# Two row tiles' transposes moved to DMA, with four smaller moves, in a kernel of attention and a gated MLP

## The chip, the core and the metric

The kernel runs on one core of one Trainium2 chip. The metric is the device time of one execution in microseconds (us). All executions told of here were in the same, fast state. Their mean granted TensorE clock was 0.998 or more of full speed, except in the slow executions of two experiments (0.995 to 0.998), whose profiles show TensorE standing still for over 6 us. "The first chunk", "chunk 1" and so on are four pieces of 512 tokens (numbers 0 to 3), each of four row tiles of 128 tokens.

## The reference, cut to what matters

```python
S, D, F = 2048, 1024, 3584
def reference(A_x, A_wqkv, A_wo, B_x, B_w_gate, B_w_up, B_w_down):
    x = A_x
    # attention: 32 heads of 32, each query looks at 8 keys spaced 2 apart
    h = x + attention(layernorm(x) @ A_wqkv) @ A_wo
    n = layernorm(h)
    return h + ((n @ B_w_gate) * (n @ B_w_up)) @ B_w_down
```

## The kernel before

The matrix products run back to back on TensorE. What they need is made by the other engines: layer norm on VectorE (`bn_stats`, then a normalization) with the reciprocal deviation from two small ScalarE instructions (`rs` in the traces); the transposed normalized rows `lnT` either through TensorE (`transpose_on_array`) or by a transposing DMA. The products' results land in PSUM tiles out of a pool of eight, and ScalarE copies each one out (`sg`).

```python
psum = ctx.enter_context(tc.tile_pool(name="psum", bufs=8, space=PSUM))
...
class Norm1:                                  # chunks 1, 2, 3
    def stat(self, t):
        stats(xtiles[self.c][t], self.mv4, t)         # VectorE
        rstd_of(self.mv4, self.rs4, t, t + 1)         # ScalarE: "rs"
    def norm(self, t):
        self.lns[t] = normalize(xtiles[self.c][t], self.mv4, self.rs4, t)
    def transpose(self, t):
        ...
        nc.sync.dma_start_transpose(lnTs[c][:, :, bass.ts(t, 128)], self.lns[t][:])
    def transpose_on_array(self, t):
        ...                                   # 8 TensorE transposes, then 2 copies PSUM -> lnT

def rows_gen(n, on_array):
    for t in range(6):
        if t < 4:
            n.stat(t)
            yield 1.5
        if 0 < t < 5:
            n.norm(t - 1)
            yield 0.55
        if t > 1 and on_array:
            n.transpose_on_array(t - 2)
            yield 0.45
...
def first_norm(t):                            # chunk 0, in two halves
    lns[t] = lnp.tile([128, D], BF, tag="ln", name=f"ln0_{t}")
    for i in range(2):
        cols = bass.ts(i, 512)
        nc.vector.tensor_scalar(lns[t][:, cols], x0[t][:, cols], mv0[:, t, 0:1], rs0[:, t:t + 1],
                                ALU.subtract, ALU.mult)
...
def evac_qkv(c, m, ps):
    sg = t1k.tile([128, HB + TC], BF, tag="t1k", name=f"sg{c}_{m}")
    nc.scalar.copy(sg[:, HB:HB + TC], ps[:])  # frees a PSUM tile
    ...
```

Side work such as the statistics is laid between the product groups by a small scheduler when the program is built: `bg.add(generator, ready)` lets a generator start once the planned time passes `ready`. The plan fixes the order of instructions on each engine; at run time each engine works in that order (ScalarE's 10 us of idling, shown further down, are an example). The stretch that will matter is this one.

```python
qkv(0, range(1, 4))
load_qk(0)                                    # query, then key rows of chunk 0, by GpSimd's DMA
bg.finish(rows2)
for t in range(4):
    norm1[2].transpose(t)                     # chunk 2, SyncE's DMA
xtiles[3] = load_x(3, "x", nc.sync)           # rows of chunk 3
pump(6)
bg.add(stats_gen(norm1[3]), bg.now + 6.0)     # their statistics
start_attention(0)
qkv(1, range(4))
```

The pair product near 520 us works from sums of weights (`sw`, out of the scaled weights `ws`) and of activations (`prodx`, out of `lnT`); the last stage, near 710 us, converts and subtracts f16 cells before the last down products.

```python
retire(1)
activation_sums(l2, l3, dn["px"])
weight_sums(0, nc.vector)
...
for k in range(NP):                           # NP = 14 cells of 128x512
    nc.vector.tensor_tensor(HF["21"][k], HF["11"][k], HF["21"][k], ALU.subtract)
for k in range(NP):
    nc.vector.tensor_tensor(HF["11"][k], S1[k], HF["11"][k], ALU.subtract)
sub(t2h, down["b22"], t1h)
```

## Time and profile before

| | before |
|---|---|
| time, median of 3 runs | 779.04 us (778.85 to 779.19) |
| span of the profiled execution | 777.6 us |
| TensorE busy | 770.7 us (99%) |
| VectorE, ScalarE, GpSimd busy | 614.9, 473.8, 142.3 us |
| TensorE idle inside the span | 6.9 us |

With TensorE busy 99% of the span, the other engines' shares say nothing by themselves. The list of TensorE's waits is the place to start, and each wait is then read in the timeline: a line there gives the start, the length, the engine, the source line (L), the operation, out<-in, and in brackets how long the engine had stood idle and what released it. One thing about those brackets was learned only later and is used below: a 512-column matmul is recorded as 0.38 us long, but in a full row the next one starts 0.22 us after it, so an idle time after a matmul leaves out 0.16 us of what was lost.

### The profile page before, as it was taken

The page shows a single profiled execution, that of the slowest core. Times are in us where ns is not written, and L with a number is a line of the kernel's source. Part 1 is how long each engine was busy: PE and PEld are TensorE (multiplying, and loading weights), DVE is VectorE, ACT ScalarE, POOL GpSimd, SP SyncE. Part 2 cuts the span into 40 slices and gives each one's busy share as a digit, 9 for nine tenths or more (in the row PEclk, how much of TensorE's full clock was granted, in tenths as well). Part 3 has the DMA queues.
Part 4 walks back from the last instruction along what each step waited for, and adds up shares of the span by engine and source line. Part 5 has one row for each costly group of instructions (what it writes and reads, how often), then busy time and mean ns, then how long its engine had stood idle before and what let it go on. Part 6 is the DMA issues. An engine that isn't in the chain of part 4 may idle for free.

```text
span 777.6 us, 10495 instructions
## 1 busy us (share of the span) xinstructions
PE 770.7 (99%) x3707; PEld 355.1 (46%) x3707; DVE 614.9 (79%) x805; ACT 473.8 (61%) x1029; POOL 142.3 (18%) x152
## 2 busy tenths in 40 slices
PE   8999999999999999999999999999999999999998
PEld 6544444444444444444444444444444444444444
DVE  6619999999899999999988989985553444579862
ACT  4627445323476661976769899746677677788240
POOL 0000000010000200002000001008778687600000
PEclk9999999999999999999999999999999999999999
DMA  8999693895965868867645384744332423730001
GB/s 275 258 217 222 158 291 88 255 305 130 338 205 167 269 228 239 267 225 259 207 150 192 120 298 121 162 96 111 106 97 67 109 62 101 248 131 28 1 27 55
DMA packets 181605, 133.86 MB, mean 172 GB/s; under 512 B 79024, under 2 KB 174384, under 8 KB 179504
## 3 DMA queue, kind: packets, MB, share of 16 engines
q1 hardware_dynamic: 176912, 110.12, 50.1%
q0 software_dynamic: 3584, 22.02, 8.1%
q10 hardware_dynamic: 1056, 1.05, 0.4%
q8 instruction: 29, 0.48, 0.3%
q14 instruction: 24, 0.20, 0.1%
HBM read 104.86 MB, written 22.02 MB: 163 GB/s over the span
## 4 chain that ended last, share of the span: by engine, by line
PE 88%; DVE 9%; DMA 1%; ACT 1%; issue 0%; SPq 0%; ACTq 0%; DVEq 0%
PE ps L392 20%; PE pg L392 12%; PE pu L392 12%; PE dx L787 6%; PE pz L680 6%; PE acc L626 6%; PE py L680 6%; PE px L680 6%; PE wo L513 4%; PE pv L680 3%; PE dy L787 3%; DVE h L834 1%; DMA w_qkv<-in_A_wqkv_dram 1%; PE ps L353 1%; PE ex L787 1%; DVE prodx L780 1%
## 5 line engine op out<-in xcount | busy, mean ns | idle before, releaser
L392 PE MATMUL ps<-lnT,w_qkv 128*128 128x512 bf16 x736 | 159.8, 379 | 0.0
L392 PEld LDWEIGHTS <-w_qkv 128*128 128x128 bf16 x736 | 71.8, 98 | 86.0 <-issue 0.3
L392 PE MATMUL pg<-lnT,w_wg 128*128 128x512 bf16 x448 | 105.8, 379 | 0.0
L392 PE MATMUL pu<-lnT,w_wu 128*128 128x512 bf16 x448 | 105.8, 379 | 0.0
L304 ACT CAST sg<-ps 128x512 bf16<-128x512 f32 x96 | 54.8, 590 | 52.7 <-PE ps L392 50.0
L475 DVE TENSOR_TENSOR pv<-vD,at 128x4096 bf16<-128x4096 bf16 x32 | 72.5, 2287 | 0.3
L432 DVE TENSOR_TENSOR prod<-qD,kD 128x4096 bf16<-128x4096 bf16 x32 | 72.3, 2284 | 0.1
L680 PEld LDWEIGHTS <-sw 128*128 128x128 f16 x448 | 43.8, 98 | 54.3 <-issue 1.7
L392 PEld LDWEIGHTS <-w_wg 128*128 128x128 bf16 x448 | 43.8, 98 | 52.9
L392 PEld LDWEIGHTS <-w_wu 128*128 128x128 bf16 x448 | 43.8, 98 | 52.9
L596 ACT CAST us<-pu 128x512 bf16<-128x512 f32 x56 | 33.2, 593 | 40.5 <-PE pu L392 40.4
L680 PE MATMUL px<-lnT,ws 128*128 128x512 bf16 x224 | 55.2, 379 | 0.0
L680 PEld LDWEIGHTS <-ws 128*128 128x128 f16 x336 | 32.9, 98 | 39.6
L626 PE MATMUL acc<-w_wd,gs 128*128 128x512 bf16 x224 | 48.5, 379 | 0.0
L487 POOL DMA_DIRECT2D od<-oD x4 | 2.2, 544 | 252.8 <-DVE oD L485 162.5
L661 POOL TENSOR_TENSOR sw<-ws 128x512 f16<-128x512 f16 x26 | 30.0, 1153 | 85.4 <-PE py L680 78.2
L185 ACT ACTIVATE rs<-mv,eps 128x1 f32<-128x1 f32 (+1 forms) x25 | 7.4, 297 | 52.6 <-DVE mv L182 49.2
L591 ACT CAST gs<-pg 128x512 bf16<-128x512 f32 x56 | 32.9, 587 | 10.7 <-PE pg L392 8.7
L434 DVE TENSOR_TENSOR prod<-prod 128x4096 bf16<-128x4096 bf16 x16 | 36.6, 2288 | 0.3
L541 ACT ACTIVATE junkd<-w_wd 128x512 bf16<-128x512 bf16 x56 | 34.3, 618 | 0.0
L626 PEld LDWEIGHTS <-gs 128*128 128x128 bf16 x224 | 21.9, 98 | 26.4
L697 ACT COPY py<-px 128x512 f32<-128x512 f32 x28 | 16.0, 570 | 26.2 <-PE px L680 26.2
(312 smaller groups left out, 1400.5 us busy)
## 6 DMA issues: line engine op xcount, KB each, us to landing
w_wg<-in_B_w_gate_dram SPq DMA_DIRECT2D x14, 1024.0 KB, 6.7
w_wu<-in_B_w_up_dram SPq DMA_DIRECT2D x14, 1024.0 KB, 5.4
w_wd<-in_B_w_down_dram SPq DMA_DIRECT2D x8, 896.0 KB, 8.8
w_pair<-in_B_w_gate_dram SPq DMA_DIRECT2D x14, 512.0 KB, 4.1
w_pair<-in_B_w_up_dram SPq DMA_DIRECT2D x14, 512.0 KB, 5.4
w_wo<-in_A_wo_dram SPq DMA_DIRECT2D x6, 1024.0 KB, 8.1
w_qkv<-in_A_wqkv_dram SPq DMA_DIRECT2D x5, 1024.0 KB, 9.1
kd<-sg SPq DMA_DIRECT2D x32, 144.0 KB, 3.0
```

The costliest lines, as they stand in the source:

```text
L304: nc.scalar.copy(sg[:, HB:HB + TC], ps[:])
L392: nc.tensor.matmul(ps[:], lhsT=wt[:, ko, bass.ts(j, 128)], rhs=rhs[:, ko, :], start=(ko == 0), stop=(ko == KO - 1))
L432: nc.vector.tensor_tensor(prod[:, j], qD[:], kD[:, :, o:o + SUB], ALU.mult)
L434: nc.vector.tensor_tensor(prod[:, :, 0:16], prod[:, :, 0:16], prod[:, :, 16:32], ALU.add)
L475: nc.vector.tensor_tensor(pv[:, j], vD[:, :, o:o + SUB], at[:, w, None, :].to_broadcast((128, DH, SUB)), ALU.mult)
L513: nc.tensor.matmul(ps[:], lhsT=oTs[c][:, kk, t, :], rhs=wts["wo", c, hf][:, kk, :], start=(kk == 0), stop=(kk == KO - 1))
L541: nc.scalar.activation(junk, src, ACTF.Abs, accum_out=self.l1[:, k:k + 1])
L591: nc.scalar.copy(gs[:], pg[:])
L596: nc.scalar.copy(us[:], pu[:])
L626: nc.tensor.matmul(acc[t][:], lhsT=hT[f][:, bass.ts(t, 128)], rhs=wts["wd", c, hf, b][:, j, :], start=(f == 0), stop=(f == NF - 1))
L680: nc.tensor.matmul(ps[:], lhsT=lhs[:, ko, :], rhs=rhs[:, ko, :], start=(fresh and ko == 0), stop=(ko == 3), skip_group_check=not fresh)
L787: nc.tensor.matmul(ps[:, bass.ds(lo, n)], lhsT=lhs[k][:, bass.ts(q, 128)], rhs=rhs[k][:, bass.ds(lo, n)], start=(fresh and k == 0), stop=( ...
```

## The change

Its intent is to take work and waits off TensorE's path at four places: sixteen transposes at 28 us, the first chunk's norm, the first pair product, and the last stage. Part 3 of the prediction is the weight half issued ahead of ScalarE's table load. The diff, with the repetitive end cut:

```diff
--- before.py
+++ after.py
@@ -222,11 +222,11 @@
         def norm(self, t):
             self.lns[t] = normalize(xtiles[self.c][t], self.mv4, self.rs4, t)
 
-        def transpose(self, t):
+        def transpose(self, t, eng=nc.sync):
             c = self.c
             if c not in lnTs:
                 lnTs[c] = lnTp.tile([128, KO, TC], BF, tag="lnT", name=f"lnT1_{c}")
-            nc.sync.dma_start_transpose(lnTs[c][:, :, bass.ts(t, 128)], self.lns[t][:])
+            eng.dma_start_transpose(lnTs[c][:, :, bass.ts(t, 128)], self.lns[t][:])
 
         def transpose_on_array(self, t):
             c = self.c
@@ -248,8 +248,11 @@
                 n.norm(t - 1)
                 yield 0.55
             if t > 1 and on_array:
-                n.transpose_on_array(t - 2)
-                yield 0.45
+                if t < 4:
+                    n.transpose_on_array(t - 2)
+                    yield 0.45
+                else:
+                    n.transpose(t - 2, nc.scalar)
 
     def stats_gen(n):
         for t in range(4):
@@ -278,8 +281,8 @@
     for t in range(4):
         load_x0(t)
     load_w0(0, 4)
+    load_w0(4, 4)
     nc.scalar.preload_act_table_set("natural_log_exp_and_others")
-    load_w0(4, 4)
     warm = t1k.tile([128, TC], BF, tag="t1k", name="warm")
     nc.vector.memset(warm[:], 0.0)
     eps = const.tile([128, 1], F32)
@@ -335,8 +338,7 @@
 
     def first_norm(t):
         lns[t] = lnp.tile([128, D], BF, tag="ln", name=f"ln0_{t}")
-        for i in range(2):
-            cols = bass.ts(i, 512)
+        for cols in (bass.ts(0, 512), bass.ts(1, 512)) if t == 0 else (slice(0, D),):
             nc.vector.tensor_scalar(lns[t][:, cols], x0[t][:, cols], mv0[:, t, 0:1], rs0[:, t:t + 1],
                                     ALU.subtract, ALU.mult)
 
@@ -977,8 +979,8 @@
         nc.vector.tensor_tensor(et[:], p5t[:, q, :], hs1[2 + q][:, 512:1024], ALU.add)
         result(1, hs1[2 + q], 2 + q, 1, ex[q], dn["inv"], et)
     retire(1)
+    weight_sums(0, nc.vector)
     activation_sums(l2, l3, dn["px"])
-    weight_sums(0, nc.vector)
     for q in range(2):
         dprod(ey[q], q, EF["12"], fcells(dn["22"]), False)
         nc.vector.tensor_tensor(p5t[:, q, :], p5t[:, q, :], hs1[q][:, 512:1024], ALU.add)
@@ -991,7 +993,8 @@
     for i in range(4):
         ht = hp.tile([128, D], BF, tag="h", name=f"hq_h{i}")
         h23 += [ht[:, 0:TC], ht[:, TC:2 * TC]]
-    for ht in (att.tile([128, KO, TC], BF, tag="oT", name="hq_o"), dn["lx"], dn["kx"], dn["vx"]):
+    rooms = (att.tile([128, KO, TC], BF, tag="oT", name="hq_o"), dn["lx"], dn["kx"])
+    for ht in rooms:
         h23 += [ht[:, k, :] for k in range(KO)]
 
 
@@ -1048,22 +1051,27 @@
     for q in range(4):
         nc.scalar.activation(ps_y[q][:], ps_x[q][:], ACTF.Copy, scale=sh)
     HF = {k: [f16(a) for a in HA[k]] for k in HA}
-    for k in range(NP):
-        to_f16(HF["22"][k], HA["22"][k], sh)
-        to_f16(HF["21"][k], HA["21"][k], sh)
+
+    GA = {k: HA[k][0:8] + [ht[:, r::4, :] for ht in rooms] for r, k in enumerate(("11", "21", "12", "22"))}
+    GF = {k: [f16(a) for a in GA[k]] for k in GA}
+    NG = len(GA["11"])
+    for k in range(NG):
+        to_f16(GF["22"][k], GA["22"][k], sh)
+        to_f16(GF["21"][k], GA["21"][k], sh)
     S1 = fcells(down["b11"])
-    for k in range(NP):
-        to_f16(HF["11"][k], HA["11"][k], sh, nc.scalar)
+    G1 = S1[0:8] + [f16(down["b11"][1][:, 2 * i + 1:2 * i + 3, :]) for i in range(3)]
+    for k in range(NG):
+        to_f16(GF["11"][k], GA["11"][k], sh, nc.scalar)
     conv_down(down["b22"], nc.scalar)
-    for k in range(NP):
-        nc.vector.tensor_tensor(S1[k], HF["21"][k], HF["22"][k], ALU.add)
+    for k in range(NG):
+        nc.vector.tensor_tensor(G1[k], GF["21"][k], GF["22"][k], ALU.add)
     for q in range(4):
         dprod(ps_x[q], q, HA["12"], fcells(down["b21"]), False)
         result(2, hs2[q], q, 0, ps_x[q], scale_d.inv, None)
-    for k in range(NP):
-        nc.vector.tensor_tensor(HF["21"][k], HF["11"][k], HF["21"][k], ALU.subtract)
-    for k in range(NP):
-        nc.vector.tensor_tensor(HF["11"][k], S1[k], HF["11"][k], ALU.subtract)
+    for k in range(NG):
+        nc.vector.tensor_tensor(GF["21"][k], GF["11"][k], GF["21"][k], ALU.subtract)
+    for k in range(NG):
+        nc.vector.tensor_tensor(GF["11"][k], G1[k], GF["11"][k], ALU.subtract)
     sub(t2h, down["b22"], t1h)
     p5 = []
     for q in range(4):
@@ (cut: HF["12"] likewise becomes GF["12"], over NG groups)
```

> **What bounds the kernel now.** I began with the first part of the page, the busy times, and then asked for the waits of TensorE alone, because the kernel looked as if one engine fills it.
>
> ```profile
> span 777.6 us, 10495 instructions
> PE 770.7 (99%) x3707; PEld 355.1 (46%) x3707; DVE 614.9 (79%) x805; ACT 473.8 (61%) x1029; POOL 142.3 (18%) x152
> ...
> PE 88%; DVE 9%; DMA 1%; ACT 1%; issue 0%; SPq 0%; ACTq 0%; DVEq 0%
> ```
>
> TensorE is busy for 770.7 of 777.6 us. The whole pool of idle time is 6.9 us (0.9% of the span), so no change that only removes waits can gain 2%. The chain of waits puts 9% on VectorE, and that can only be a place where VectorE ends a TensorE wait. The list of TensorE's waits says where:
>
> ```profile
> PE warm_ps L298 <- DVE warm L284: 1.2, 1, 1.2
> PE pv L680 <- DVE h L792: 1.1, 2, 0.9
> PE ps L353 <- ACT lnT L348: 0.3, 1, 0.3
> PE pt L347 <- DVE ln L340: 0.3, 1, 0.3
> PE ps L353 <- DMA w_qkv<-in_A_wqkv_dram: 0.3, 1, 0.3
> PE dy L787 <- DVE prodx L780: 0.3, 1, 0.3
> ```
>
> Three places are recoverable: the first token chunk (three waits of 0.3), the first pair product at about 520 us (1.1), and the last stage at 727 us (0.3 shown). The 1.2 at the start is not touched. From the end of the last matmul to the end of the span there are over 3 us of store, also untouched. So I read the timeline closely at exactly these places, and at 24 to 30 us, where the transposes of chunk 1 sit.
>
> **What the Trainium skill says.** (1) "DMA: Bandwidth & Descriptors", section "Silent corruption: two transposing streams in flight at once": transposes issued from the ScalarE queue and from the SyncE queue must not be in flight together; the later stream has to wait for the earlier one. Here the first SyncE transpose starts at 41.08 us, some 10 us after the new ScalarE ones would be issued, so if a wait is there it should be met already. The before trace has one stream only and cannot test this. (2) Same page, "Issuing engines are not separate DMA queues": another issuing engine buys no bandwidth, only sequencer time. So I give the choice of queue no transfer gain. (3) "Perfetto Trace Analysis", section "Optimizing Scalar/DVE Operations": about 60 ns overhead per VectorE instruction on SBUF, grouping helps where the engine is saturated, and splitting lets work end sooner where it only causes bubbles on others. The trace agrees on the size: near the end a pair of 128x512 f16 subtractions occupies 0.67 us from its start to the next pair's, and a 128x1024 one 0.61 us. (4) "TensorE: Matmul & The Clock Gate", "Part 4: PE-mode transpose" gives about 275 ns for a 128x128 transpose in one kernel. The trace differs in what a transpose costs in a row: eight of them push the next matmul by 0.45 us, 56 ns each; the measurement decides.
>
> **Part 1: two row tiles leave TensorE.** The chain of waits has these pieces:
>
> ```profile
> 24.72 1.73 PE ps L392 x8
> 26.90 1.73 PE ps L392 x8
> 28.62 0.89 PE ptb L238 x16
> ```
>
> Tiles 0 and 1 cost 0.45 us each between groups (24.72 + 1.73 = 26.45, next group at 26.90) and stay. Tiles 2 and 3 are the 16 transposes of 0.89 us, and they go: −0.89 us, directly on TensorE, which does not wait again before 519 us. Their four PSUM copies go too (two of 0.42 on VectorE, two of 0.59 on ScalarE), off the path. In their place ScalarE issues two DMA transposes. Estimated from SyncE's, each takes about 1.28 us to issue and 3.1 to 3.3 us to land:
>
> ```profile
> L229 SPq DMA_TRANSPOSE lnT<-ln x8: 1258/1280/5748, 41.1 to 94.9; - x8
> ...
> DMA to landing us min/median/max: 3.1/3.3/9.7
> ```
>
> The last norm of chunk 1 is done at 27.8 us and ScalarE has a cast and a copy before it, so issue from about 29.3, the second about 30.6, landed by about 34. The first chunk 1 matmul comes after twelve groups of 1.73 from 17.21 and the transposes: 17.21 + 20.7 + 0.45 + 0.45 + 0.89 = 39.7 before, 38.8 after. Slack of about 5 us.
>
> **Part 2: the first chunk's norm in one piece for tiles 1 to 3.** The normalization feeds the array's transposes:
>
> ```profile
> 13.88 0.73 DVE L340 TENSOR_SCALAR ln<-x,mv,rs 128x512 bf16<-128x512 bf16 x2 [0.86 <-ACT rs L186]
> 14.35 0.55 PEld L347 LDWEIGHTS <-ln 128*128 128x128 bf16 x8
> ...
> 14.79 1.07 ACT L348 COPY lnT<-pt 128x512 bf16<-128x512 bf16 x2 [0.94 <-PE pt L347]
> ```
>
> One half takes 0.41 us; 13.88 + 0.41 + 0.06 of signalling = 14.35, exactly when the transposes start. So they start on the first half. Tile 2 is alike: 11.44 + 0.41 + 0.06 = 11.91. One 128x1024 norm took 0.54 (median of the same operation in chunk 1 and later), so each transpose start moves by +0.13. This goes round a loop (transposes, ScalarE copies, rstd on ScalarE, next norm), so tile 3 gets it twice, +0.26, and tile 1 adds about +0.05. The later transposes run closer together, as they no longer wait for a second half, but the last products need the copy of tile 3. I put the end of this stage +0.3 us later. VectorE is freed 0.19 earlier per tile, which buys nothing: the norms wait for ScalarE's rstd (0.86 above).
>
> **Part 3: the second half of the first weight block issued ahead of the table load.** Before, the two ScalarE-queue issues began at 0.75 and 1.27 and the table load was dispatched at 1.24; only some 0.03 to 0.05 us lies between them. The 0.3 us wait for that block may shrink by that, but tile 1's norm is then the bound. Value 0. The table load ends 0.5 later, near 3.0, and its first user is at 5.60.
>
> **Part 4: weight sums before activation sums.** The waits of the first pair product:
>
> ```profile
> 507.38 3.69 ACT L654 ACTIVATE ws<-w_pair,sbgu 128x4096 f16<-128x4096 bf16 x1
> ...
> 511.90 1.23 DVE L672 TENSOR_TENSOR prodx<-lnT,lnT 128x2048 f16<-128x2048 bf16 x1 [2.19 <-DMA out_dram<-h]
> ...
> 516.57 0.69 DVE L661 TENSOR_TENSOR sw<-ws 128x1024 f16<-128x1024 f16 x1
> ...
> 520.69 1.02 PE L680 MATMUL pv<-prodx,sw 128*128 128x512 f16 x4 [0.88 <-DVE h L792]
> ...
> 522.81 1.02 PE L680 MATMUL pv<-prodx,sw 128*128 128x512 f16 x4 [0.23 <-DVE h L792]
> ```
>
> VectorE idles 2.19 us until 511.90 for the last transposed row tile (I read the out_dram name as a mislabel: the sums read lnT). The weight sums need only ws, ready at 507.38 + 3.69 = 511.07. Both groups together took 519.11 − 511.90 = 7.21 us without a gap; put the other way round they start at 511.10 and end at 518.31. (The activation sums then start near 513.6, well after their tiles have landed.) VectorE is 0.80 us ahead. The h additions that free the PSUM banks follow at once, so TensorE's first pv moves from 520.69 to 519.89; its px products end at 517.92 + 1.89 = 519.81, so it can take it. Gain 0.80. The second wait, 0.23, is between two things that both move and stays. So the 1.1 us of wait falls to about 0.3, not to zero.
>
> **Part 5: wider conversions and differences at the end.** Each of 14 instructions becomes 11, three of them 128x1024. Only what VectorE does between its release at 713.16 and the last-stage differences counts: two passes, six merged pairs, 0.67 − 0.61 = 0.06 each, −0.36 us. The second difference that TensorE needs then ends at 726.8 rather than 727.17, and TensorE, which could have gone at about 726.6, moves by the same 0.36. The scalings on ScalarE save more, but nothing on the path waits for them.
>
> Sum: −0.89 + 0.3 + 0 − 0.80 − 0.36 = −1.75 us, so 779.04 becomes about 777.3.
>
> **The rivals.** First, the transposes land late. One of the SyncE transposes took 5.75 us to issue and 9.7 to land, beside the key load. If ScalarE meets such a one at 30.6, it lands at 40.3 and TensorE waits 1.5 us at chunk 1, turning part 1 into a loss: total about 779 to 779.5. For it: DMA share in slices 2 and 3 is 9. Against: that stall came after a GpSimd load had begun, and here the query load is issued only at 30.97. Second, ScalarE is held for 2.6 us (or 6) by the issues, its PSUM evacuations come late and TensorE runs out of banks. Eight banks against 1.73 us a group leave several groups; only a 6 us hold would be close. Third, VectorE absorbs the early gain: it is over 95% busy from 80 to 350 us, and if it can't follow, the early 0.6 us returns as a longer wait at 520. Against: at 455 us VectorE waits 1.21 us for TensorE, so it has room to follow. If it did happen, 777.9. Fourth, the norm loop has slack that I don't see and part 2 costs nothing: 777.0.
>
> **Range and chances.** The working gives 777.3; the rivals spread from 777.0 to 779.5, the likelier ones to 778.0, and runs of before differ by 0.3. I say 776.5 to 778.4. Faster or slower by 2% means 15.6 us: more than all idle time on one side, and far more than any rival on the other.
>
> **What would show it.** No transposes of tiles 2 and 3 on TensorE at 28.6, and chunk 1 starting near 39 without a wait for a DMA (else rival one). In the first stage the transposes of tiles 2 and 3 starting 0.6 us after their norm instead of 0.47, and the stage's end about 0.3 later; if it isn't, part 2 is wrong. At 520 us, minus the shift, the first pv wait near 0.1 and the second still there; if the first stays at 0.88, part 4 is wrong. At 727 the difference wait shorter, with pairs at 0.61; if a strided pair takes 0.67, part 5 is zero. TensorE's busy time should fall by about 0.9. A time over 779 would refute the sum.

## The result, and the profile after

The changed kernel took 777.9 us (median of 4 runs, 777.57 to 778.13), against 779.1 for the kernel before (4 runs, 778.85 to 779.19). Ratios here and below are the mean time of one kernel's fast runs over the mean of the other's in the same rounds, so not quite the ratio of the medians: 0.9985, 95% interval 0.9969 to 1.0001. All results were correct. That is a gain of about 1.2 us, of the 1.75 us predicted. The interval reaches just past 1, but the slowest run of the changed kernel lies under the fastest of the kernel before. The span of the profiled execution fell by 1.5 us.

The busy times on the page, and TensorE's waits (us in total, times, longest), of the kernel after:

```profile
span 776.1 us, 10428 instructions
PE 770.0 (99%) x3691; PEld 354.4 (46%) x3691; DVE 612.0 (79%) x782; ACT 471.6 (61%) x1021; POOL 142.5 (18%) x152
```

```profile
PE warm_ps L301 <- DVE warm L287: 1.2, 1, 1.2
PE ps L394 <- ACT sg L307: 0.7, 1, 0.7
PE ps L355 <- ACT lnT L350: 0.5, 1, 0.5
PE pv L682 <- DVE h L794: 0.2, 1, 0.2
```

TensorE lost 16 matmuls (3707 to 3691) and 0.7 us of busy time, as it should. The pair wait fell from 1.1 to 0.2 and the last stage's wait is gone from the list. But the second line is new: at 60 us TensorE waits 0.7 us for a PSUM copy (`sg`) by ScalarE. No such wait was in the list of before. (L394, L307 are L392, L304 of before.)

**The new wait.** First the timeline of before around it, then that of after: SyncE's issue of chunk 3's rows, the first statistics of them, ScalarE's first copy after them, and, in after, TensorE's restart.

```profile
51.08 2.59 SPq L202 DMA_DIRECT2D x<-in_A_x_dram  x4
55.17 1.29 DVE L181 BATCH_NORM_STATS2 st<-x 128x6 f32<-128x512 bf16 x2 [16.81 <-DMA x<-in_A_x_dram]
59.96 0.57 ACT L304 CAST sg<-ps 128x512 bf16<-128x512 f32 x1
```

```profile
45.83 3.73 SPq L202 DMA_DIRECT2D x<-in_A_x_dram  x4
54.99 1.29 DVE L181 BATCH_NORM_STATS2 st<-x 128x6 f32<-128x512 bf16 x2 [15.99 <-DMA x<-in_A_x_dram]
...
56.56 0.29 ACT L185 ACTIVATE rs<-mv,eps 128x1 f32<-128x1 f32 x1 [10.06 <-DVE mv L182]
59.78 0.57 ACT L307 CAST sg<-ps 128x512 bf16<-128x512 f32 x1
60.39 1.89 PE L394 MATMUL ps<-lnT,w_qkv 128*128 128x512 bf16 x8 [0.71 <-ACT sg L307]
```

Read it from the bottom. TensorE restarts at 60.39 because a copy that began at 59.78 freed a PSUM tile. ScalarE had stood idle for 10.06 us before 56.56, although products were there to be copied: next in its program order was `rs`, which needs VectorE's statistics, and these waited for the rows of chunk 3, landed at 54.99. Three tiles' `rs` come ahead of the next copy. So the copy starts 59.78 − 54.99 = 4.79 us after the rows, and TensorE 5.40 us after them. Eight PSUM tiles carry TensorE for 8 x 1.73 = 13.8 us without a copy, which is just what the kernel before needed: it had no listed wait. But its timeline holds the trace of one. This is TensorE's line in a window around 60.6 us of before:

```profile
60.22 0.73 PE L392 MATMUL ps<-lnT,w_qkv 128*128 128x512 bf16 x2
```

Two such matmuls in a full row take 0.59 us (0.216 from start to start, and 0.38 for the last), so the second of these, at 60.58, started about 0.14 us late: less than the 0.16 us that the list leaves out. The kernel before already arrived at 60 us with nothing to spare, and the kernel after, 0.9 us earlier, runs into the wait. SyncE issued the rows 5.25 us earlier than before (51.08 to 45.83), but they landed only 0.18 us earlier.

**The transposes.** They were predicted to land by about 34 us, with 5 us of slack. Two lines of the timeline of after: the two issues by ScalarE, and the VectorE instruction that needs a source buffer of theirs back. Then, from the view of the tile `lnT`, the issue-to-landing times of the four transposes in the stretch from 28 to 42 us (two of them ScalarE's).

```profile
29.43 2.76 ACTq L229 DMA_TRANSPOSE lnT<-ln  x2
38.45 0.55 DVE L190 TENSOR_SCALAR ln<-x,mv,rs 128x1024 bf16<-128x1024 bf16 x1 [1.40 <-DMA lnT<-ln]
```

```profile
DMA to landing us min/median/max: 3.4/3.5/7.4
```

The issue was as estimated (29.3, 2.76 us for two). The slower one took 7.4 us to land; issued at 30.87, it was there at 38.3, and TensorE used it at 38.80. The slack was 0.5 us, not 5.

**The other parts.** The norm of the first chunk's last tile and the transposes fed by it; the first weight sum and the first pair product; one of the merged pairs and the last stage's first product with a difference. All are timeline lines; the first fence has the three of before for the last stage, the second those of after.

```profile
716.50 0.75 DVE L1064 TENSOR_TENSOR hq_o<-hq_o 128x512 f16<-128x512 f16 x2
...
725.28 1.46 PE L787 MATMUL dy<-prodx,hq 128*128 128x512 f16 x6
...
727.22 0.38 PE L787 MATMUL dy<-prodx,hq_h 128*128 128x512 f16 x1 [0.26 <-DVE prodx L780]
```

```profile
13.73 0.55 DVE L342 TENSOR_SCALAR ln<-x,mv,rs 128x1024 bf16<-128x1024 bf16 x1 [1.18 <-ACT rs L186]
14.33 0.45 PEld L349 LDWEIGHTS <-ln 128*128 128x128 bf16 x8 [0.17 <-DVE ln L342]
...
510.90 0.69 DVE L663 TENSOR_TENSOR sw<-ws 128x1024 f16<-128x1024 f16 x1 [1.39 <-ACT ws L656]
...
519.70 1.02 PE L682 MATMUL pv<-prodx,sw 128*128 128x512 f16 x4
...
715.50 0.68 DVE L1072 TENSOR_TENSOR hq_o<-hq_o 128x1024 f16<-128x1024 f16 x1
...
724.04 1.46 PE L789 MATMUL dy<-prodx,hq 128*128 128x512 f16 x6
```

The transposes start 0.60 us after their norm (14.33 − 13.73) where before it was 0.47. The weight sums start when `ws` is there, and the first pair product has no listed wait left. A pair of subtractions occupies 0.60 us to the next one's start (716.10 follows 715.50) where it was 0.67.

A ledger of TensorE's way, from the same timelines, shows where the time went. Each row is a start on TensorE.

| TensorE starts | before | after | after minus before |
|---|---|---|---|
| the first chunk's second weight block | 17.21 | 17.19 | −0.02 |
| chunk 1 | 39.71 | 38.80 | −0.91 |
| the pair stage's first products (px) | 517.92 | 517.74 | −0.18 |
| the second pv product | 522.81 | 521.81 | −1.00 |
| the second group of dy products | 728.73 | 727.31 | −1.42 |

So 0.73 us of the 0.91 won at 28 us was given back before 517 us; the pair stage gave 0.82 and the last stage 0.42. The first row needs care: in this one profile of after the first row tile arrived 0.38 us earlier than in the profile of before (first statistic at 3.65 against 4.03), which hides a cost of part 2. ("The first stage" below is the time from that first statistic to the second weight block.)

### The profile page after: what moved, and what is told of

Read it like the earlier page. It is cut to its first block, busy times and chain, and to the rows that moved or that the text cites. A ratio compares the mean times of both kernels' runs of the same rounds, so it can differ in the third digit from the quotient of the medians.

```text
span 776.1 us, 10428 instructions
## 1 busy us (share of the span) xinstructions
PE 770.0 (99%) x3691; PEld 354.4 (46%) x3691; DVE 612.0 (79%) x782; ACT 471.6 (61%) x1021; POOL 142.5 (18%) x152
## 4 chain that ended last, share of the span: by engine, by line
PE 86%; DVE 9%; DMA 2%; ACT 1%; SPq 1%; issue 0%; ACTq 0%; DVEq 0%
PE ps L394 18%; PE pu L394 12%; PE pg L394 12%; PE dx L789 6%; PE pz L682 6%; PE acc L628 6%; PE py L682 6%; PE px L682 6%; PE wo L515 4%; PE pv L682 3%; PE dy L789 3%; DMA x<-in_A_x_dram 1%; DVE st L181 1%; DVE h L836 1%; DMA w_qkv<-in_A_wqkv_dram 1%; PE ps L355 1%
## 5 line engine op out<-in xcount | busy, mean ns | idle before, releaser
L394 PE MATMUL ps<-lnT,w_qkv 128*128 128x512 bf16 x736 | 159.7, 379 | 0.7 <-ACT sg L307 0.7
L394 PEld LDWEIGHTS <-w_qkv 128*128 128x128 bf16 x736 | 71.9, 98 | 87.0 <-issue 1.0
L394 PE MATMUL pg<-lnT,w_wg 128*128 128x512 bf16 x448 | 105.8, 379 | 0.0
L394 PE MATMUL pu<-lnT,w_wu 128*128 128x512 bf16 x448 | 105.8, 379 | 0.0
L307 ACT CAST sg<-ps 128x512 bf16<-128x512 f32 x96 | 54.8, 590 | 51.2 <-PE ps L394 48.5
L394 PEld LDWEIGHTS <-w_wu 128*128 128x128 bf16 x448 | 43.8, 98 | 52.9
L394 PEld LDWEIGHTS <-w_wg 128*128 128x128 bf16 x448 | 43.8, 98 | 52.9
L682 PEld LDWEIGHTS <-ws 128*128 128x128 f16 x336 | 32.9, 98 | 39.6
```

Source lines behind the costliest of these rows:

```text
L394: nc.tensor.matmul(ps[:], lhsT=wt[:, ko, bass.ts(j, 128)], rhs=rhs[:, ko, :], start=(ko == 0), stop=(ko == KO - 1))
L682: nc.tensor.matmul(ps[:], lhsT=lhs[:, ko, :], rhs=rhs[:, ko, :], start=(fresh and ko == 0), stop=(ko == 3), skip_group_check=not fresh)
```

## The experiments

The first theory, named A in the texts on record, is the one just read: the new wait at 60 us is set by the landing of chunk 3's rows, through ScalarE's fixed order and the eight PSUM tiles, so that whatever TensorE gains before 60 us is paid back there. Its rivals are that the transposes held ScalarE or landed late, so that part 1 itself is the loss (the prediction's first two rivals), and that a gain at 60 us would be lost again later, to VectorE, whatever was done at 60. The texts say what each expects. Twelve kernels ran, in four sets, each set on one chip together with the kernel before. Edits are to the kernel after unless stated. The "median" is the run's, with the kernel before in the same rounds behind it. An interval that contains 1 means that the times alone do not show a difference; there the argument rests on the profile, which is of one execution.

### All four tiles on TensorE again (part 1 undone)

```diff
-                if t < 4:
-                    n.transpose_on_array(t - 2)
-                    yield 0.45
-                else:
-                    n.transpose(t - 2, nc.scalar)
+                n.transpose_on_array(t - 2)
+                yield 0.45
```

> The changed kernel with all four row tiles of chunk 1 transposed on TensorE again, everything else changed. Theory A (the 0.9 us saved at 28 us is paid back as a new 0.7 us wait of TensorE at about 60 us, because the x rows of chunk 3 land at about 55 us whatever TensorE does and ScalarE's queue stands behind them): the wait at 60 us vanishes, chunk 1 starts 0.9 us later, and the total is only about 0.2 us above the changed kernel (span about 776.3). Theory B (the DMA transposes are worth their full 0.9 us and the missing part went elsewhere): about 0.9 us above (span about 777.0).

Measured: median 778.12 us (before 778.94), ratio 0.9991 (0.9979 to 1.0003), span 776.3. The wait at 60 us is gone from the list, and px starts at 517.88, 0.14 us later than in after. So with part 1, whose direct saving is 0.89 us, TensorE is only 0.14 us ahead at px. Theory A holds here.

### Chunk 3's statistics planned later

```diff
-    bg.add(stats_gen(norm1[3]), bg.now + 6.0)
+    bg.add(stats_gen(norm1[3]), bg.now + 12.0)
```

> The changed kernel with the row statistics of chunk 3 placed later in the program (three more PSUM evacuations stand ahead of them in ScalarE's queue). Theory A: the 0.7 us wait at 60 us vanishes, since the banks are emptied before ScalarE meets the late rows; span 776.1 becomes about 775.4. Theory B (TensorE would have waited there for something else, such as weights): the wait stays near 0.7 under another name and the span stays near 776.1.

Measured: median 777.71 us (before 778.94), ratio 0.9983 (0.9971 to 0.9995), span 775.7. The timeline of ScalarE shows what changed: its last copy ahead of the blocked `rs`, and that `rs`.

```profile
51.38 0.59 ACT L307 CAST sg<-ps 128x512 bf16<-128x512 f32 x1 [1.14 <-PE ps L394]
56.60 0.30 ACT L185 ACTIVATE rs<-mv,eps 128x1 f32<-128x1 f32 x1 [4.63 <-DVE mv L182]
```

The rows landed as late as ever (first statistic at 55.03), but three more copies went ahead of `rs`, ScalarE stood blocked for 4.63 us where it had been 10.06, and TensorE has no wait at 60. px starts at 517.16, 0.58 us earlier than in after, although the first stage ran 0.29 us later. The order of ScalarE's queue is the cause; the transposes' issue hold of 2.76 us, which this kernel has too, is not. (The medians of this kernel and of after, 777.71 and 777.9 us, are too close to tell apart; the reading is from the profiles.)

### Chunk 3's rows loaded ahead of chunk 2's transposes

```diff
+    xtiles[3] = load_x(3, "x", nc.sync)
     for t in range(4):
         norm1[2].transpose(t)
-    xtiles[3] = load_x(3, "x", nc.sync)
```

> The changed kernel with the loads of the x rows of chunk 3 issued ahead of chunk 2's four DMA transposes on the SyncE queue (about 40 us in place of 46). Theory A: the rows land before 55 us, at about 48 to 50, the wait at 60 us vanishes, span about 775.4. Rival C (they land at 55 because the DMA engines are full from 42 to 55 us, not because they are issued late): first rows land later than 53, and the wait shrinks little, span 775.9 or more.

Measured: median 777.53 us (before 778.94; one run of five at 779.26), ratio 0.9985 (0.9972 to 0.9998), span 775.9. The rows, issued at 40.72, now land at 44.31, and there is no wait at 60: rival C fails. In this profile the first row tile arrived late (first statistic at 4.24), which put the first stage 0.55 us behind that of after; px still starts 0.31 us ahead. So time freed at 60 us does reach the pair stage; it is not lost on the way. There is a price: SyncE's four transposes, now beside the key load, took 16.34 us to issue.

### The norm in halves again (part 2 undone)

```diff
-        for cols in (bass.ts(0, 512), bass.ts(1, 512)) if t == 0 else (slice(0, D),):
+        for cols in (bass.ts(0, 512), bass.ts(1, 512)):
```

> The changed kernel with the first chunk's norm of tiles 1 to 3 in two halves again. If the one-piece norm costs 0.3 us in the first stage as predicted: block 1 of chunk 0 starts at about 16.9 instead of 17.19 us. Under theory A the wait at 60 us then grows by the same amount (0.7 to 1.0) and the span does not change (776.1); under theory B the span falls to 775.8. If the one-piece norm costs nothing, block 1 starts at 17.2 in both.

Measured: median 778.06 us (before 778.94), six runs from 777.1 to 781.15, ratio 0.9993 (0.998 to 1.0006), span 776.8. The expectation that the wait at 60 would grow missed. The stage did get shorter: from the first statistic to the second weight block it took 13.22 us, against 13.54 in after. But the transposes landed later still, and TensorE waited for them at chunk 1. The timeline line of TensorE's restart, and the issue-to-landing times from the view of the tile in the same stretch as above:

```profile
40.35 1.89 PE L394 MATMUL ps<-lnT,w_qkv 128*128 128x512 bf16 x8 [1.80 <-DMA lnT<-ln]
```

```profile
DMA to landing us min/median/max: 4.3/4.5/9.7
```

This is the prediction's first rival, in one profile: 9.7 us to land. TensorE came late to chunk 1, so it found nothing to wait for at 60.

### The table load ahead again (part 3 undone)

```diff
-    load_w0(4, 4)
     nc.scalar.preload_act_table_set("natural_log_exp_and_others")
+    load_w0(4, 4)
```

> The changed kernel with the table load between the two weight loads again. Six runs so far: the last packet of the first weight block ended at 8.47 us in the kernel before and at 7.99 to 8.31 in the five with the new order, while the first statistic began at 4.03 before and at 3.55 to 4.24 in those five. If the order matters: last packet after 8.4 here. If it is only scatter of the start (the prediction's value 0): anywhere between 8.0 and 8.5. The span should differ from the changed kernel (776.1) only by the shift of the first statistic, under 0.5 us.

Measured: median 777.77 us (before 778.86), ratio 0.9984 (0.9971 to 0.9996), span 775.2. The first weight block's last packet came at 8.02 us; over all profiles it came at 7.93 to 8.51 with the new order and at 8.02 to 8.47 with the old. No effect of part 3 can be seen. The short span, 0.9 us under that of after where less than 0.5 was expected, has another cause: chunk 3's rows happened to land at 53.93, a microsecond earlier than in after, and there was no wait at 60.

### The weight sums alone (before, with part 4)

```diff
-    activation_sums(l2, l3, dn["px"])
     weight_sums(0, nc.vector)
+    activation_sums(l2, l3, dn["px"])
```

> The kernel before with only the weight sums put ahead of the activation sums. Prediction's part 4: TensorE's waits at the first pair product fall from 1.1 to about 0.3 us, span 777.6 becomes 776.8, time 0.8 us below before. Rival: the early 0.2 us of the changed kernel made it, and alone the waits stay above 0.6.

Measured: median 778.3 us (before 778.86), 0.56 us lower and not 0.8, ratio 0.9991 (0.9977 to 1.0005), span 776.5. The pair wait is 0.2 as in after. From px to the second pv product it took 4.09 us, against 4.89 in before and 4.07 in after.

### The wider conversions alone (before, with part 5)

```diff
-    for ht in (att.tile([128, KO, TC], BF, tag="oT", name="hq_o"), dn["lx"], dn["kx"], dn["vx"]):
+    rooms = (att.tile([128, KO, TC], BF, tag="oT", name="hq_o"), dn["lx"], dn["kx"])
+    for ht in rooms:
 ... and the loops over NG groups, as in the change
```

> The kernel before with only the last stage's merged instructions (11 in place of 14). Prediction's part 5: six merged pairs on VectorE's path at 0.06 us each, the wait for the difference at 727 us goes, span 777.6 becomes 777.2, time 0.4 us below before. Rival (the strided pair of rows runs no faster than two single rows): no change.

Measured: median 778.54 us (before 778.86), ratio 0.9995 (0.9982 to 1.0007), span 776.6. From the second pv product to the second dy group it took 205.50 us, as in after; in before and with the weight sums alone it took 205.92. The last stage is worth 0.42 us, whatever the rest does.

### The transposes from SyncE's queue

```diff
-                    n.transpose(t - 2, nc.scalar)
+                    n.transpose(t - 2)
```

> The changed kernel with the two DMA transposes of chunk 1 issued from SyncE's queue in place of ScalarE's. If the queue matters (SyncE's stands behind stores of the key rows that wait for ScalarE): the transposes are issued later than 29.4 us, land later than 38.8 and TensorE waits 1 us or more at chunk 1; span 777 or more. If only the collision with GpSimd's query load from 30.6 us on matters: they land between 37 and 40 us as from ScalarE, and the span is 776 to 777.

Measured: median 778.17 us (before 778.86), ratio 0.9994 (0.9981 to 1.0006), span 776.3. SyncE issued at 30.20 and needed 2.71 us for the two, and they landed at about 39.6: TensorE waited 0.3 us for them at 39.65 and 0.3 at 60. The second expectation held; the queue matters little here.

### Rows first, and the key load ahead of the query load

The transposes of the kernel after were in flight beside GpSimd's query load (issued at 30.60). To take that load out of their way without a new wait, chunk 0's key load, which can only start near 43 us, was put ahead of it, with the rows-first edit as well.

```diff
-        nc.gpsimd.dma_start(qD[:], qd[c].rearrange("c g d s -> (c g) d s"))
-        nc.gpsimd.dma_start(kD[:], kd[c].rearrange("c g d s -> (c g) d s"))
+        for dst, src in ((kD, kd), (qD, qd)) if c == 0 else ((qD, qd), (kD, kd)):
+            nc.gpsimd.dma_start(dst[:], src[c].rearrange("c g d s -> (c g) d s"))
```

> The changed kernel with the x rows of chunk 3 loaded ahead of chunk 2's transposes, and for chunk 0 the key load issued ahead of the query load on GpSimd's queue. So far the last of the two chunk 1 transposes ended its transfer at 37.7 to 39.7 us, always behind the query load that GpSimd issued at 30.5 to 31 us, and TensorE needs them at 38.8 to 39.3. If that collision is what makes them late: with the query load gone until about 44 us, the transposes end before 34.5 us, and TensorE waits at neither 39 nor 60 us; span 775.4 or less, and no run above 778. If something else holds them: they still end after 37.

Measured: median 784.32 us (before 778.9), six runs from 777.44 to 786.51, ratio 1.0055 (1.0026 to 1.0084), span 783.8. Half of it came as hoped. In the stretch from 28 to 42 us, where only ScalarE's two transposes are, they landed in 3.1 to 3.5 us, against up to 7.4 and 9.7 beside the query load. But SyncE's four, now beside both GpSimd loads, held its queue for 25 us. The issue-to-landing line for the tile in that stretch, and SyncE's line in the timeline:

```profile
DMA to landing us min/median/max: 3.1/3.3/3.5
```

```profile
42.16 25.16 SPq L229 DMA_TRANSPOSE lnT<-ln  x4
```

The last two weight blocks of the projection were issued behind them at 67.38, and TensorE waited 6.7 us for one at 73 us. The stop cost more than its length: afterwards the granted clock was 0.50 for 3.4 us (73.3 to 76.7), and the first 14 matmuls took 4.85 us where 14 in a full row, 0.216 us apart, take 3.18, so 1.67 us more.

### The same, with the norm in halves

The edit is the two above together.

> As the run before it, and the first chunk's norm of tiles 1 to 3 in halves again. The first stage (first statistic to block 1) is 13.2 us in place of 13.5; with neither wait left at 39 and 60 us the 0.3 us should now reach the end, which it didn't in the run with halves alone: span 775.1 or less from the same start, median about 0.3 us under the run before it and about 2 us under before.

Measured: median 778.82 us (before 778.9), six runs from 777.29 to 785.41, ratio 1.0018 (0.9988 to 1.0049), span 783.6, with a wait of 6.1 us for the weight block in the profile. The times fall in two groups, four from 777.29 to 779.12 and two above 784, so the collision is met in some executions and not in others; the median says little here.

### The kernel after, once more

No edit; it ran in the same rounds as the two before it.

> The changed kernel itself once more, in these rounds. The wait at 60 us comes or goes with the landing of chunk 3's first x rows (none when the first statistic on them began at 53.9, 0.7 at 55.0): expected between 0 and 1 us here, by 0.65 us per us of landing at the most, and the median 777.6 to 778.1.

Measured: median 778.35 us (before 778.9), five runs from 777.88 to 778.67, ratio 0.9992 (0.998 to 1.0004), span 776.4. The rows landed at 55.31 and the wait at 60 was listed with 0.9 us. The wait lies in the expected range, the median above the expected 777.6 to 778.1. By the medians the gain of the change is thus 1.2 us in one set of rounds and 0.55 us in the other.

### The query load held until the transposes have landed

Two one-column copies on GpSimd read the transposed tiles into a place that the query load overwrites, so the load waits for them; the statistics are planned later and the norm is in halves.

```diff
+        if c == 0:
+            for t in (2, 3):
+                nc.gpsimd.tensor_copy(qD[:, 0, t:t + 1], lnTs[1][:, 0, 128 * t:128 * t + 1])
         nc.gpsimd.dma_start(qD[:], qd[c].rearrange("c g d s -> (c g) d s"))
...
-    bg.add(stats_gen(norm1[3]), bg.now + 6.0)
+    bg.add(stats_gen(norm1[3]), bg.now + 12.0)
```

> The changed kernel with three things: GpSimd's query load for chunk 0 waits until both chunk 1 transposes have landed (two one-column copies on GpSimd that read them), the statistics of chunk 3 placed later, and the norm of tiles 1 to 3 in halves. Theory: the transposes land near 34 us, TensorE waits at neither 39 nor 60 us, the first stage is 13.2 us, and the whole 0.9 us of part 1 reaches the end: span 775.1 for a first statistic at 3.65, median about 776.9, 2 us under before and 1 us under the changed kernel. Rival: the query load, moved by 3 us, runs into the key load or the stores of the key rows as in the two runs with the loads reordered; then a wait for weights or for the query rows appears and the span is above 776.

Measured: median 777.35 us (before 778.98), five runs from 777.06 to 777.99, ratio 0.9982 (0.9968 to 0.9996), span 775.4, where a median of 776.9 and a span of 775.1 were expected. The transposes had landed by 33.4 and 34.1 us, when GpSimd's copies ran, and neither chunk 1 nor 60 us has a wait. TensorE is ahead by 1.6 us of before at 60 us, and now it meets the prediction's third rival: VectorE, almost without a gap since 60 us, brings a row tile late at 190 us (it was busy for 126.2 of the 130 us in between). The first two of TensorE's waits:

```profile
PE warm_ps L301 <- DVE warm L287: 1.2, 1, 1.2
PE pg L394 <- DMA lnT<-ln: 0.5, 1, 0.5
```

This has the lowest median of all, but its interval overlaps those of the kernel after and of the two simpler edits (statistics later, rows first). It beats before, about 1.6 us by the medians. That it beats after is likely from the traces and not shown by the times.

### All runs in one account

The traces allow a stricter test of theory A than the waits alone. From TensorE's restart at 60.39 to px at 517.74 the kernel after takes 457.35 us. If nothing between adds a wait, px starts 457.35 us after the later of two times: TensorE's own arrival, or the first statistic of chunk 3's rows + 5.40 us (the bound, from after). The own arrival is the start of the second weight block plus 42.33 us with DMA transposes (taken from the profile with the table load undone: 516.82 − 457.35 − 17.14), or 43.22 with all on TensorE (from that of the weight sums alone: 517.62 − 457.35 − 17.05). The two differ by 0.89 us, the price of the sixteen transposes. This account was made after the runs, and three of them gave its constants; the nine below did not.

| kernel | own arrival | rows + 5.40 | px computed | px measured |
|---|---|---|---|---|
| before | 17.21 + 43.22 = 60.43 | 60.57 | 517.92 | 517.92 |
| part 1 undone | 17.30 + 43.22 = 60.52 | 60.21 | 517.87 | 517.88 |
| statistics later | 17.48 + 42.33 = 59.81 | not in the way | 517.16 | 517.16 |
| rows first | 17.74 + 42.33 = 60.07 | not in the way | 517.42 | 517.43 |
| part 2 undone | 16.78 + 1.96 + 42.33 = 61.07 | 61.12 | 518.47 | 518.47 |
| part 5 alone | 16.78 + 43.22 = 60.00 | 60.16 | 517.51 | 517.52 |
| SyncE's queue | 17.58 + 0.45 + 42.33 = 60.36 | 60.56 | 517.91 | 517.91 |
| after, once more | 17.50 + 42.33 = 59.83 | 60.71 | 518.06 | 518.06 |
| query load held | 16.65 + 42.33 + 0.66 = 59.64 | not in the way | 516.99 | 517.00 |

(Each listed wait of TensorE enters with the 0.16 us that the list leaves out: 1.80, 0.29 and 0.50 become 1.96, 0.45 and 0.66; the last one falls at 190 us.) Nine starts come out within 0.01 us. The two runs with the key load first are not in the table, since TensorE also ran slowly after its stop: with the listed wait plus 0.16 us (6.90 and 6.30) and the slow matmuls (1.67 us, and 15 matmuls in 5.70 us in place of 3.40, or 2.30 us) the sums for px are 525.44 and 525.29, which is what was measured. Two readings follow that no wait list gives. The kernel before already stood on the bound: its own arrival is 60.43 and the rows allowed 60.57, which is the 0.14 us seen in its timeline. And of everything won ahead of 60 us only the movement of the bound counts, here 60.57 to 60.39, or 0.18 us.

## Why the prediction was right, and where it was not

The time, 777.9 us, lies in the stated range of 776.5 to 778.4 us; the middle, 777.3, was 0.6 us too low. Parts 2 to 5 came about as described. Part 1, the largest term, mostly did not, and the range was wide enough to hold that. It is chance that the prediction's third rival names exactly 777.9: the growing wait at 520 us that it describes did not come (0.2 us there). By its own steps:

- **What bounds the kernel: right.** TensorE at 99%, and places with waits of less than a microsecond to gain.
- **Part 1, −0.89: the saving is there, most of it did not last.** Chunk 1 starts 0.91 us earlier and the two natural arrivals differ by 0.89. The failing step is the sentence that put it "directly on TensorE, which does not wait again before 519 us". That was true of the list of before and not of the changed kernel: before already stood on the bound at 60 us. The step read "no wait" as "slack", and the list had left out a stop of 0.14 us at 60.58. The estimate of the landing, "about 34", failed too, with 38.3 measured. The first rival was argued away because the query load "is issued only at 30.97"; it was issued at 30.60, and even at 30.97 it falls within the second transpose's own estimated flight, from 30.6 to about 34. Taking the load out of the way brought the slower landing down from 7.4 and 9.7 us to 3.5 (key load first) and 4.5 (query load held). The rival's total was also misadded: 777.3 with a wait of 1.5 us is 778.8, not 779 to 779.5. The kernel after got by with 0.5 us of slack; with the norm in halves it did not (1.8 us).
- **Part 2, +0.3: right.** From the first statistic to the second weight block the six profiles with halves took 13.10 to 13.22 us and the eight with one piece 13.50 to 13.65. The transposes start 0.60 us after their norm instead of 0.47, as said. Its cost, like part 1's gain, is mostly swallowed by the bound at 60 us.
- **Part 3, 0: right**, as far as a scatter of 0.5 us lets one see.
- **Part 4, −0.80: right.** −0.82 in the ledger, −0.80 alone. In the profile of part 5 alone the old order took 4.67 us and not 4.89, as the last row tile landed earlier (VectorE's wait for it ended at 511.27 and not 511.90); the gain is thus 0.6 to 0.8 us from one execution to another.
- **Part 5, −0.36: right, slightly small.** −0.42, as a merged pair saves 0.07 us and not 0.06. TensorE's lines show two delays before, 0.24 us at 725.28 and 0.43 us at 727.22 (both with the 0.16 us that the list leaves out; the first is not listed); after, one of 0.25 us is left, at 725.80.
- **The second rival** had the right victim (PSUM tiles run out as ScalarE is held) and the wrong cause: not the 2.76 us of issuing, but a 10.06 us wait for rows. **The third** was met in one run, at 190 us and not at 520, once TensorE came 1.6 us earlier.
- **The rule on two transposing streams** (point 1 of what the skill says) was kept in every profile and tested in none: ScalarE's last transpose landed at about 40.2 us at the latest (part 2 undone), and SyncE's first one was issued there at 40.92, when its stores were done. All results were correct.

Parts 1 to 3 were booked with −0.59 us in sum and brought −0.18; parts 4 and 5 were booked with −1.16 and brought −1.24. In the traces that is −1.42; the median times gave −1.2 and, in the second set of rounds, −0.55. Why the kernel after spreads from set to set is open: the landings of the rows (first statistics from 53.93 to 55.72 over the profiles that issue them behind the transposes) and of the transposes vary by more than a microsecond and each moves the end, which fits, but a profile shows one execution only. Open too is why rows issued 5 us earlier land at the same time; that the key load of 1152 KB, issued at 43.56, is in flight speaks for a collision with it, and so does that the rows landed 3.6 us after their issue at 40.72, ahead of the key load, and 9.2 us after that at 45.83. But no run took the key load away alone.

## What to carry to other kernels

Before a gain on the busiest engine is booked, look for places downstream where it arrives just in time: an engine that stands idle for 10 us in front of a tiny instruction while its next task is to free a buffer is such a place, even if no wait is listed. Compute the bound there (landing plus the fixed chain behind it) beside the engine's own arrival, and book only the smaller movement. A small instruction that waits for a late transfer belongs as late as it can go in the queue of an engine that also empties buffers; here that took away the wait at 60 us, one place in one kernel.

## What the Trainium skill lacked or had wrong

- "DMA: Bandwidth & Descriptors", "Rules for kernel authors", says that a transpose next to ordinary DMAs needs nothing. For correctness no run here contradicts it; for time it lacks a figure for a transpose beside other DMAs. Beside GpSimd's loads a 128x1024 transpose took up to 7.4 and 9.7 us to land, with the query load out of the way 3.1 to 3.5 us, and four of them held SyncE's queue for 25.16 us beside two such loads, against 5.59 us in after.
- The same page, "Issuing engines are not separate DMA queues", agrees with the runs: ScalarE's issue took 2.76 us and SyncE's 2.71 us for the same two transposes, and the time changed little. It calls the issue time usually small beside the transfer; here it is about 1.3 us of the 3.1 to 3.5 us that an undisturbed transpose takes from issue to landing.
- "TensorE: Matmul & The Clock Gate", "Part 4: PE-mode transpose": about 275 ns per transpose stands there, as a duration. The records here last 0.22 us each, but overlap: in a row of sixteen one costs 0.89 us / 16 = 56 ns of TensorE's time. That section lacks this second figure for a transpose.
- "Perfetto Trace Analysis", "Optimizing Scalar/DVE Operations", has both halves of what happened, and its dividing line, whether the engine is saturated, held: grouping saved 0.07 us per pair in the last stage (0.67 to 0.60), where VectorE was busy for 14.04 of 14.30 us in before, and cost 0.3 to 0.4 us in the first stage, where it was busy for 10.98 of 13.20 us and splitting fed TensorE earlier. Nothing is lacking there.
- "PSUM — Partial Sum Buffer", "Engine vs sequencer instructions", has the strict order of ScalarE's queue, but no page that was read names that order as a cause of PSUM running out: ScalarE idle for 10.06 us before one 128x1 instruction, TensorE stopped 0.7 us at the end of it.
